# Exponent-bit terms of an attention kernel written by GpSimd in halves instead of by VectorE

## Chip, cores, metric

One core of one Trainium2 chip. The metric is device time of one execution, in microseconds, as a median over runs; shorter is better. A profile is one execution whose span is about 1.7 us shorter than the timed figure. All runs were in the fast state except the second of e4 (963.3 us, slow); the two single probe runs, e1 and e8, have no known state.

Terms: TensorE does the matmuls, ScalarE (ACT in the profiles) the exponentials and tanh, VectorE (DVE) and GpSimd (POOL) elementwise work. PSUM is the memory in which TensorE leaves its results, SBUF the working memory; to evict is to copy from PSUM to SBUF. The granted clock is the share of TensorE's full clock that the throttle let it have.

## The reference

A layer norm feeds two branches, and their sum is added to the input: attention with 16 heads of 28 columns over 2048 tokens, and a gated MLP (448 to 1792 to 448).

```python
def reference(A_x, A_wqkv, A_wo, B_x, B_w_gate, B_w_up, B_w_down):
    # _A_ref: q, k, v from xn @ wqkv; p = softmax(q k^T * Dh**-0.5); (p v) @ wo
    # _B_ref: (gelu(xn @ w_gate) * (xn @ w_up)) @ w_down
    x = A_x
    xn = _layernorm(x, axis=-1)
    return x + _A_ref(xn, A_wqkv, A_wo) + _B_ref(xn, B_w_gate, B_w_up, B_w_down)
```

## The kernel before

The scores of attention are made in 512 slots (two heads, 128 keys, 512 queries each), and each needs an exponential. ScalarE does 464 of them. The other 48 slots, two to a group, are done by VectorE with a trick: write `w = 128 * scale * log2(e) * score` as float16, then add a constant and convert to uint16; the bits, read as bfloat16, are a rough power of two. Five such terms with five constants are summed by TensorE, which multiplies each by the values. A group so costs VectorE two conversions from PSUM (`w`) and five terms.

```python
SHIFTS = (-2.74189, -2.62767, -2.43854, -2.23824, -1.98187)
...
    # keys of the groups in a sweep (two groups each), and the block that takes their terms
    D_AT = (((0, 4, 4), (8, 12, 12)), ((0, 4, 4), (8, 12, 12)), ((0, 4, 0), (5, 9, 0)))
...
    def emit_w(k):
        ...
        nc.vector.tensor_scalar(out=w_tiles[g][1][:, 2 * i * QT : 2 * (i + 1) * QT],
            in0=s_tiles.pop(k)[:], scalar1=128.0 * SCALE * LOG2E, scalar2=None, op0=ALU.mult)
...
    def emit_term(g, j):
        n, w = w_tiles[g]
        c = 128.0 * (127.0 + SHIFTS[j])
        if j == len(SHIFTS) - 1:
            bits = w[:].bitcast(U16)              # the last term overwrites w
        else:
            n = l_free.pop(0)[1]
            bits = ltile(n, [P, 4 * QT], U16, "t")[:]
        nc.vector.tensor_scalar(out=bits, in0=w[:], scalar1=c, scalar2=None, op0=ALU.add)
        ...
```

The order of all instructions comes from a planner inside the kernel. When the kernel is built, it plays the engines forward with a clock for each and with fixed costs, and emits whatever could start first. On the chip only the order and the data waits remain. TensorE fills planned gaps with filler matmuls (`jp`). VectorE also evicts PSUM and runs five gelu steps for each of 28 pieces of the MLP. Those five, all from SBUF to SBUF:

```python
T_EXP = 903; T_SWITCH = 100; PE_TO = 416; S_TO = 432; ACT_TO = 162; DVE_TO = 136; C_TS = 345; C_TERM = 608  # ns
...
            nc.vector.tensor_mul(st["a"][:], g[:], g[:])                     # two SBUF inputs
            nc.vector.tensor_scalar(out=st["a"][:], in0=st["a"][:], ...)     # one
            nc.vector.tensor_mul(st["a"][:], st["a"][:], g[:])               # two
            # tanh on ScalarE
            nc.vector.tensor_scalar(out=st["a"][:], in0=st["a"][:], ...)     # one
            nc.vector.tensor_mul(ht[:], st["a"][:], gu[:])                   # two
```

The softmax here doesn't subtract the row's maximum and nothing guards it: scores larger than these inputs give would overflow.

## Time and profile before

| | before |
|---|---|
| median of the first three runs | 487.17 us (487.15 to 488.54) |
| profiled span, granted TensorE clock | 485.5 us, 0.993 |
| ScalarE: first, last start of 492 large instructions | 13.8, 473.1 us |
| ScalarE: median spacing of starts | 904 ns |
| ScalarE: sum of spacing above 905 ns | 15.2 us, of it 12.8 us after 140 us |

The last three rows are worked out from the start times in the trace. ScalarE is the pacemaker: at 904 ns from start to start, the 491 intervals alone take 444 us.

From the page of the kernel before: busy time by engine, then the span in 40 slices (the busy share of a slice in tenths), then the chain of waits by engine.

```profile
PE 462.5 (95%) x3530; PEld 160.6 (33%) x3530; DVE 407.4 (84%) x728; ACT 463.4 (95%) x505; POOL 19.5 (4%) x74
...
DVE  6788999787469999999778999999986999776574
ACT  4899999999999999999999999999999999999992
POOL 4602020000000000000000000000000000000000
PEclk9999999999999999999999999999999999999997
...
PE 56%; DVE 28%; ACT 9%; issue 4%; POOL 1%; DMA 1%; DVEq 0%; ACTq 0%; POOLq 0%
```

ScalarE (ACT) is full from the second slice to the last but one, GpSimd (POOL) is empty from the eighth, and VectorE (DVE) is nearly full in several stretches. The groups view of the kernel before has line, engine, operation, output<-input, shapes and count, then busy us and mean ns of one, then idle time before it and its releaser:

```profile
L584 ACT ACTIVATE e<-st 128x1024 bf16<-128x1024 f32 x464 | 433.2, 1066 | 5.9 <-PE st L572 4.8 <-ACT e L584 0.3
L615 DVE TENSOR_SCALAR t<-w 128x2048 uint16<-128x2048 f16 x96 | 63.6, 684 | 0.2
L373 DVE TENSOR_TENSOR gl<-gl,g 128x1024 bf16<-128x1024 bf16 x28 | 19.2, 684 | 0.3
L615 DVE TENSOR_SCALAR w<-w 128x2048 uint16<-128x2048 f16 x24 | 16.6, 690 | 0.6
L367 DVE TENSOR_SCALAR gl<-gl 128x1024 bf16<-128x1024 bf16 x28 | 11.7, 418 | 0.1
```

The second and fourth lines are the work to be moved: 80.2 us. ScalarE idles before an exponential for only 5.9 us in all; the rest of its 15.2 us must be short delays hidden in overlapping durations. The table of stretches of the kernel before, before and after the first VectorE score groups, gives start:end, length, then the busy time of each engine:

```profile
13.80:140.00 126.20, 123.68 (x892) 45.52 (x891) 99.47 (x210) 125.98 (x137) 12.38 (x48) 1.00 0.21 59
140.00:475.00 335.00, 322.58 (x2556) 108.22 (x2555) 296.17 (x476) 329.72 (x356) 0.00 (x0) 1.00 0.11 31
```

The columns are PE, PEld, DVE, ACT, POOL, then granted clock, DMA share and GB/s. VectorE is busy 296 of 335 us in the second stretch.

### The profile page before, as it was taken

How to read it: one execution, taken by the hardware profiler on the slowest of the kernel's cores; microseconds unless marked ns; L12 is line 12 of the kernel's file. 1: busy time of each engine (PE TensorE's matmuls, PEld its weight loads, DVE VectorE, ACT ScalarE, POOL GpSimd, SP SyncE). 2: the span in 40 equal slices, each digit the busy share in tenths (PEclk: the TensorE clock that was granted, in tenths of full speed). 3: DMA queues.
4: the chain of work that ended last, by engine and by line, in shares of the span. 5: the costliest groups of instructions: out<-in, count | busy, mean ns of one | idle time of the engine just before them, and what ended most of it. 6: DMA issues, size and time to landing. Idle time of an engine off the chain costs nothing.

```text
span 485.5 us, 9277 instructions
## 1 busy us (share of the span) xinstructions
PE 462.5 (95%) x3530; PEld 160.6 (33%) x3530; DVE 407.4 (84%) x728; ACT 463.4 (95%) x505; POOL 19.5 (4%) x74
## 2 busy tenths in 40 slices
PE   8999999999999999999999999999999999999994
PEld 3343333333333332333333233323333333233221
DVE  6788999787469999999778999999986999776574
ACT  4899999999999999999999999999999999999992
POOL 4602020000000000000000000000000000000000
PEclk9999999999999999999999999999999999999997
DMA  6910112120011220120002022111001030000001
GB/s 165 311 36 20 39 39 61 36 57 20 2 42 38 77 61 19 40 58 21 1 1 60 28 70 62 40 53 40 3 1 39 30 87 3 1 2 1 2 1 38
DMA packets 41052, 20.71 MB, mean 43 GB/s; under 512 B 8240, under 2 KB 41008, under 8 KB 41008
## 3 DMA queue, kind: packets, MB, share of 16 engines
q1 hardware_dynamic: 40112, 19.68, 15.0%
q8 instruction: 27, 0.44, 0.4%
q10 hardware_dynamic: 896, 0.44, 0.3%
q14 instruction: 17, 0.14, 0.1%
HBM read 18.09 MB, written 1.84 MB: 41 GB/s over the span
## 4 chain that ended last, share of the span: by engine, by line
PE 56%; DVE 28%; ACT 9%; issue 4%; POOL 1%; DMA 1%; DVEq 0%; ACTq 0%; POOLq 0%
PE st L572 13%; PE gups L407 12%; PE ot L622 11%; PE op L469 10%; ACT e L584 8%; DVE t L615 4%; PE pp L309 4%; DVE w L594 4%; DVE g L393 3%; PE jp L985 3%; DVE gu L398 2%; PE pv L320 1%; DVE otsb L644 1%; DVE gl L363 1%; DVE st L211 1%
## 5 line engine op out<-in xcount | busy, mean ns | idle before, releaser
L584 ACT ACTIVATE e<-st 128x1024 bf16<-128x1024 f32 x464 | 433.2, 1066 | 5.9 <-PE st L572 4.8
L572 PE MATMUL st<-qT,kT 28*128 28x512 bf16 x1024 | 123.6, 383 | 2.9 <-ACT e L584 2.5
L622 PE MATMUL ot<-e,va 128*32 128x512 bf16 x928 | 92.4, 384 | 2.0 <-DVE gu L398 0.6
L572 PEld LDWEIGHTS <-kT 28*128 28x128 bf16 x1024 | 34.8, 91 | 110.5 <-issue 107.7
L594 DVE TENSOR_SCALAR w<-st 128x1024 f16<-128x1024 f32 x48 | 58.4, 1219 | 6.8 <-PE st L572 6.4
L615 DVE TENSOR_SCALAR t<-w 128x2048 uint16<-128x2048 f16 x96 | 63.6, 684 | 0.2
L407 PE MATMUL gups<-xnT,wu 112*128 112x512 bf16 x224 | 60.5, 380 | 2.3 <-DVE otsb L644 0.9
L407 PE MATMUL gups<-xnT,wg 112*128 112x512 bf16 x224 | 60.2, 381 | 0.6 <-DVE otsb L640 0.3
L622 PEld LDWEIGHTS <-va 128*32 128x32 bf16 x1408 | 34.1, 94 | 66.9 <-issue 55.6
L469 PE MATMUL op<-wd_sb,ht 128*128 128x448 bf16 x224 | 49.6, 354 | 0.4 <-DVE pre L497 0.2
L393 DVE CAST g<-gups 128x512 bf16<-128x512 f32 x56 | 38.2, 685 | 6.0 <-PE gups L407 5.9
L398 DVE TENSOR_TENSOR gu<-gups,g 128x512 bf16<-128x512 f32 x56 | 38.2, 685 | 3.1 <-PE gups L407 2.9
L644 DVE TENSOR_TENSOR otsb<-ot,otsb 128x512 f32<-128x512 f32 x45 | 30.8, 685 | 11.3 <-PE ot L622 10.9
L622 PE MATMUL ot<-t,va 128*32 128x512 bf16 x384 | 38.8, 384 | 0.4 <-DVE t L615 0.4
L377 ACT ACTIVATE gl<-gl 128x1024 bf16<-128x1024 bf16 x28 | 30.3, 1089 | 0.0
L407 PEld LDWEIGHTS <-wu 112*128 112x128 bf16 x224 | 19.4, 97 | 29.8 <-issue 14.7
L407 PEld LDWEIGHTS <-wg 112*128 112x128 bf16 x224 | 18.9, 97 | 28.7 <-issue 14.1
L469 PEld LDWEIGHTS <-ht 128*128 128x128 bf16 x224 | 18.9, 98 | 23.7 <-issue 10.3
L497 DVE TENSOR_TENSOR pre<-op,x 128x448 f32<-128x448 f32 x16 | 9.9, 621 | 18.0 <-PE op L469 18.0
L373 DVE TENSOR_TENSOR gl<-gl,g 128x1024 bf16<-128x1024 bf16 x28 | 19.2, 684 | 0.3
L389 DVE TENSOR_TENSOR ht<-gl,gu 128x1024 bf16<-128x1024 bf16 x28 | 19.1, 684 | 0.3
L363 DVE TENSOR_TENSOR gl<-g 128x1024 bf16<-128x1024 bf16 x28 | 19.1, 683 | 0.1
(105 smaller groups left out, 327.8 us busy)
## 6 DMA issues: line engine op xcount, KB each, us to landing
wg<-in_B_w_gate_dram SPq DMA_DIRECT2D x28, 224.0 KB
wu<-in_B_w_up_dram SPq DMA_DIRECT2D x28, 224.0 KB
out_dram<-res SPq DMA_DIRECT2D x15, 112.0 KB
wd_sb<-in_B_w_down_dram SPq DMA_DIRECT2D x1, 1568.0 KB
x<-in_A_x_dram SPq DMA_DIRECT2D x3, 448.0 KB
den<-otsb SPq DMA_DIRECT2D x60, 2.0 KB
rr<-recb SPq DMA_DIRECT2D x60, 1.0 KB
wst<-in_A_wqkv_dram SPq DMA_DIRECT2D x2, 392.0 KB
```

The source lines that it names most:

```text
L363: nc.vector.tensor_mul(st["a"][:], g[:], g[:])
L377: nc.scalar.activation(st["a"][:], st["a"][:], AF.Tanh, scale=TANH_SCALE)
L393: nc.vector.tensor_copy(g[:, k, :], ps[:])
L398: nc.vector.tensor_mul(gu[:, k, :], ps[:], g[:, k, :])
L407: nc.tensor.matmul(ps[:], lhsT=w[:, c, k * P : (k + 1) * P], rhs=xnc(Q, c), start=(c == 0), stop=(c == NDC - 1),)
L469: nc.tensor.matmul(ps[:, 0:D], lhsT=l, rhs=r, start=(n == 0), stop=(n == len(seq) - 1))
L572: nc.tensor.matmul(st[:, j * QT : (j + 1) * QT], lhsT=kT[(hg, kc // 4)][32 * hh : 32 * hh + Dh, (kc % 4) * P : (kc % 4 + 1) * P], rhs=qT[( ...
L584: nc.scalar.activation(e[:], s_tiles.pop(k)[:], AF.Exp, scale=SCALE)
L594: nc.vector.tensor_scalar(out=w_tiles[g][1][:, 2 * i * QT : 2 * (i + 1) * QT], in0=s_tiles.pop(k)[:], scalar1=128.0 * SCALE * LOG2E, scala ...
L615: nc.vector.tensor_scalar(out=bits, in0=w[:], scalar1=c, scalar2=None, op0=ALU.add)
L622: nc.tensor.matmul(ot[32 * hh : 32 * hh + 32, :], lhsT=vaug[kc][:, h * 32 : (h + 1) * 32], rhs=rhs, start=(b, hh) not in started, stop=las ...
L644: nc.vector.tensor_add(otsb[:], ot[:], otsb[:])
```

## The change

The intent: VectorE looks loaded and GpSimd idle, so GpSimd writes the terms, in halves of 1024 columns so that VectorE's gelu steps get a turn in between. The groups move to other keys of each sweep, to leave GpSimd time. The planner gets a clock for GpSimd (1030 ns for a half), does not plan a half and a gelu step at once, and several of its constants are re-tuned. The core of the diff, cut:

```diff
-T_SWITCH = 100
-PE_TO = 416
-S_TO = 432
-ACT_TO = 162
-DVE_TO = 136
+T_SWITCH = 104
+PE_TO = 430
+S_TO = 445
+ACT_TO = 180
+DVE_TO = 150
+POOL_TO = 150
+RAW = 85
+P_TERM = 1030
 ...
-    D_AT = (((0, 4, 4), (8, 12, 12)), ((0, 4, 4), (8, 12, 12)), ((0, 4, 0), (5, 9, 0)))
+    D_AT = (((0, 2, 8), (5, 8, 12)), ((0, 2, 8), (5, 8, 12)), ((0, 2, 0), (4, 6, 0)))
 ...
-    def emit_term(g, j):
+    def emit_term(g, j, i):
 ...
-        nc.vector.tensor_scalar(out=bits, in0=w[:], scalar1=c, scalar2=None, op0=ALU.add)
+        n, bits = t_tiles[g, j]
+        sl = slice(2 * i * QT, 2 * (i + 1) * QT)
+        nc.gpsimd.tensor_scalar(out=bits[:, sl], in0=w[:, sl], scalar1=c, scalar2=None, op0=ALU.add)
 ...
+    def pool_choice():          # when GpSimd's next half may start; it yields to a gelu step
+        ...
+        s = max(t, it[0], dve_lock[0])
+        d = dve_choice()
+        if d is not None and d[2][0] == 4 and d[0] < s + HOLD:
+            return None
+        return s, lambda: do_pool(it)
```

Not shown are other cost constants, the times at which gelu steps count as ready, and a rule at the end of the last block.

More of the change, by code (lines that the diff above doesn't have):

```diff
@@ L24 @@
 T_MM = 216
-T_SWITCH = 100
-PE_TO = 416
-S_TO = 432
-ACT_TO = 162
-DVE_TO = 136
+T_SWITCH = 104
[4 more added lines that the diff above has]
+POOL_TO = 150
 C_EVAC = 608
 C_TT = 600
-C_TS = 345
+C_TS = 335
+RAW = 85
 C_TERM = 608
 C_W = 1142
+P_TERM = 1030
 DMA_HOP = 5200
@@ L268 @@
     avail = {}
-    clock = {"PE": 0.0, "ACT": 0.0, "DVE": 0.0}
+    clock = {"PE": 0.0, "ACT": 0.0, "DVE": 0.0, "POOL": 0.0}
     dve_items = []
+    pool_items = []
     seq_n = [0]
@@ L275, in dve, with pool @@
         dve_items.append((cls, seq_n[0], ready, cost, f, keys))
+    def pool(ready, g, j, i):
+        seq_n[0] += 1
+        pool_items.append((ready, seq_n[0], g, j, i))
     def aux_tile(shape, dt, name):
@@ L288, in g_transpose @@
             if j == 0:
-                yield ("mm", 260)
+                yield ("mm", 268)
         yield (
-            "ev", 260, 1110, lambda: nc.vector.tensor_copy(xnT[t0 // 4][:, :, (t0 % 4) * P : (t0 % 4 + 2) * P], tp[0:DCH, :, :]),
+            "ev", 268, 1000, lambda: nc.vector.tensor_copy(xnT[t0 // 4][:, :, (t0 % 4) * P : (t0 % 4 + 2) * P], tp[0:DCH, :, :]),
             [("x", t0 // 4, t0 % 4 // 2)],
@@ L363, in f_sq @@
             nc.vector.tensor_mul(st["a"][:], g[:], g[:])
-            dve(4, 0, C_TS, f_poly)
+            dve(4, clock["DVE"] + C_TT + RAW, C_TS, f_poly)
         def f_poly():
@@ L369, in f_poly @@
             )
-            dve(4, 0, C_TT, f_arg)
+            dve(4, clock["DVE"] + C_TS + RAW, C_TT, f_arg)
         def f_arg():
@@ L383, in f_half @@
             )
-            st["half"] = True
+            st["half"] = clock["DVE"] + C_TS + RAW
             if st["gu"] == 2:
-                dve(4, 0, C_TT, f_h, [("ht", Q, pr)])
+                dve(4, st["half"], C_TT, f_h, [("ht", Q, pr)])
         def f_h():
@@ L394, in f_g @@
             if k == 1:
-                dve(4, 0, C_TT, f_sq)
+                dve(4, clock["DVE"] + C_EVAC + RAW, C_TT, f_sq)
         def f_gu(k, ps):
@@ L400, in f_gu @@
             if st["gu"] == 2 and "half" in st:
-                dve(4, 0, C_TT, f_h, [("ht", Q, pr)])
+                dve(4, clock["DVE"] + C_EVAC + RAW, C_TT, f_h, [("ht", Q, pr)])
         for w, f in ((wg, f_g), (wu, f_gu)):
@@ L605, with emit_term_dve @@
     term_ready = {}
-    def emit_term(g, j):
+    t_tiles = {}
+    NDT = 0
+    def emit_term_dve(g, j):
+        w = w_tiles[g][1]
+        n = l_free.pop(0)[1]
+        bits = ltile(n, [P, 4 * QT], U16, "t")[:]
+        nc.vector.tensor_scalar(
+            out=bits, in0=w[:], scalar1=128.0 * (127.0 + SHIFTS[j]), scalar2=None, op0=ALU.add
+        )
+        term_ready.setdefault(groups[g][2], []).append((clock["DVE"] + C_TERM + DVE_TO, g, n, bits))
+    def emit_term(g, j, i):
         n, w = w_tiles[g]
         c = 128.0 * (127.0 + SHIFTS[j])
-        if j == len(SHIFTS) - 1:
-            bits = w[:].bitcast(U16)
-        else:
-            n = l_free.pop(0)[1]
-            bits = ltile(n, [P, 4 * QT], U16, "t")[:]
-        nc.vector.tensor_scalar(out=bits, in0=w[:], scalar1=c, scalar2=None, op0=ALU.add)
-        term_ready.setdefault(groups[g][2], []).append((clock["DVE"] + C_TERM + DVE_TO, g, n, bits))
+        if i == 0:
+            if j < len(SHIFTS) - 1:
+                n = l_free.pop(0)[1]
+                t_tiles[g, j] = n, ltile(n, [P, 4 * QT], U16, "t")[:]
+            else:
+                t_tiles[g, j] = n, w[:].bitcast(U16)
+        n, bits = t_tiles[g, j]
+        sl = slice(2 * i * QT, 2 * (i + 1) * QT)
+        nc.gpsimd.tensor_scalar(out=bits[:, sl], in0=w[:, sl], scalar1=c, scalar2=None, op0=ALU.add)
+        if i == 1:
+            term_ready.setdefault(groups[g][2], []).append((clock["POOL"] + P_TERM + POOL_TO, g, n, bits))
     started = set()
@@ L829 @@
         for k in range(4):
-            ln_at_time(p0 + k, 640, lambda t=4 * g + k: ln_stats(t))
-        ln_at_time(p0 + 4, 500, lambda g=g: (ln_round(g), ln_std_newton(g)))
-        ln_at_time(p0 + 8, 180, lambda g=g: ln_rstd(g))
+            ln_at_time(p0 + k, 750, lambda t=4 * g + k: ln_stats(t))
+        ln_at_time(p0 + 4, 885, lambda g=g: (ln_round(g), ln_std_newton(g)))
+        ln_at_time(p0 + 8, 90, lambda g=g: ln_rstd(g))
         for k in range(4):
@@ L884, in do_s @@
             next_s[0] += 1
-        run_pe(start, "S", 216)
+        run_pe(start, "S", 227 if n == 2 else 222)
     def pv_choice():
@@ L896, in pv_choice @@
             best = (tr[0][0], "t")
-        if tail and not final[0] and len(sg["left"]) == 1:
-            return None
-        if sg["left"] and (sg["terms"] == 0 or len(sg["left"]) > 1):
+        if sg["left"] and not (tail and not final[0] and len(sg["left"]) == 1) and (sg["terms"] == 0 or len(sg["left"]) > 1):
             n, kc = sg["left"][0]
@@ L930, in do_pv @@
             l_free.append((start + 216 + PE_TO, n))
-            run_pe(start, "V", 216)
+            run_pe(start, "V", 226)
             return
@@ L938, in do_pv @@
             e_free[k] = start + 216 + 250
-        run_pe(start, "V", 222)
+        run_pe(start, "V", 226)
         if last:
@@ L1062, in dve_ok @@
         if isinstance(f, tuple) and f[0] == "t":
-            return f[2] == len(SHIFTS) - 1 or bool(l_free)
+            return bool(l_free)
         return True
@@ L1070, in dve_choice @@
             return None
+        if pool_run[0] <= t < pool_run[1]:
+            its = [it[:2] + (max(it[2], pool_run[1]),) + it[3:6] + (it,) if it[0] == 4 else it for it in its]
         ready = [it for it in its if it[2] <= t]
@@ L1079, in dve_choice @@
             it = min(its, key=lambda i: (i[2], i[0]))
-        return max(t, it[2]), lambda: do_dve(it)
+        return max(t, it[2]), lambda: do_dve(it), it
     def do_dve(it):
-        _, _, r, cost, f, keys = it
-        dve_items.remove(it)
-        start = clock["DVE"] = max(clock["DVE"], r)
+        cls, _, r, cost, f, keys = it[:6]
+        dve_items.remove(it[6] if len(it) > 6 else it)
+        start = max(clock["DVE"], r)
+        if cls == 4:
+            if pool_run[0] <= start < pool_run[1]:
+                start = pool_run[1]
+            dve_lock[0] = start + cost
+        clock["DVE"] = start
         end = start + cost
@@ L1093, in do_dve @@
                 if i == 1:
-                    dve(3, end, C_TERM, ("t", g, 0))
+                    dve_terms[g] = NDT
+                    for j in range(NDT):
+                        dve(4, end + RAW, C_TERM, ("t", g, j))
+                    pool(end + DVE_TO, g, NDT, 0)
             elif f[0] == "t":
-                _, g, j = f
-                emit_term(g, j)
-                terms_done[0] += 1
-                if j + 1 < len(SHIFTS):
-                    dve(3, end, C_TERM, ("t", g, j + 1))
+                emit_term_dve(f[1], f[2])
+                dve_terms[f[1]] -= 1
             else:
@@ L1108, in do_dve, with do_pool @@
         clock["DVE"] = end
+    HOLD = 300
+    dve_terms = {}
+    pool_run = [0.0, 0.0]
+    dve_lock = [0.0]
+    def pool_choice():
+        t = clock["POOL"]
+        its = [
+            it for it in pool_items if it[4] == 1 or (dve_terms[it[2]] == 0 if it[3] == len(SHIFTS) - 1 else l_free)
+        ]
+        if not its:
+            return None
+        it = min(its)
+        s = max(t, it[0], dve_lock[0])
+        d = dve_choice()
+        if d is not None and d[2][0] == 4 and d[0] < s + HOLD:
+            return None
+        return s, lambda: do_pool(it)
+    def do_pool(it):
+        pool_items.remove(it)
+        r, _, g, j, i = it
+        start = clock["POOL"] = max(clock["POOL"], r, dve_lock[0])
+        emit_term(g, j, i)
+        end = clock["POOL"] = start + P_TERM
+        pool_run[:] = [start, end]
+        j, i = j + i, 1 - i
+        if j < len(SHIFTS):
+            pool(end, g, j, i)
     def step():
@@ L1113, in step @@
             l_free.extend((0.0, n) for n in range(NL))
-        opts = [c for c in (act_choice(), pe_choice(), dve_choice()) if c is not None and c[0] < INF]
+        opts = [c for c in (act_choice(), pe_choice(), dve_choice(), pool_choice()) if c is not None and c[0] < INF]
         if not opts:
@@ L1123 @@
         pass
-    assert next_a[0] == len(a_slots) and not (todo or urgent or lazy or mid[0] or dve_items or tanh_q)
+    assert next_a[0] == len(a_slots) and not (todo or urgent or lazy or mid[0] or dve_items or pool_items or tanh_q)
     final[0] = True
@@ L1139 @@
     preload(2)
+    assert segs[-1]["terms"] == 0
     while segs[-1]["left"]:
```

## The prediction

> **What bounds the kernel now.** ScalarE. The groups view gives 464 exponentials of 128x1024, and 28 tanh. They overlap: in the timeline, consecutive starts are 904 ns apart in the median. The first starts at 13.8 us and the last at 473.1 us, so 491 intervals take 459.3 us; at 0.904 us each they would take 443.9 us. ScalarE therefore loses about 15.2 us to late inputs, of which 12.8 us lie after 140 us (where VectorE score groups begin) and 2.4 us before. Outside the stream there are 13.8 us of head and about 12 us of tail. The page shows TensorE 95% busy (closely matched, with 41 filler matmuls), VectorE 84%, GpSimd 4%. In the windows view VectorE is 88% busy from 140 to 475 us and 97 to 99% busy in 40 us stretches there. The chain of waits puts 28% on VectorE: its late evictions make ScalarE's inputs late. At 188 to 192 us VectorE runs five terms in a row, TensorE nine filler matmuls, and ScalarE idles 0.7 us.
>
> **What changes.** The counts of exponentials, tanh and useful matmuls are the same in the built program; filler matmuls fall from 41 to 5. VectorE loses 120 terms of 128x2048: 96 x 684 ns + 24 x 690 ns = 80 us. Its load after 140 us falls from 296 us to about 216 us of 335 (65%). GpSimd gains 240 halves of 128x1024. From this trace's GpSimd copies (one element 0.18 us, 448 columns 0.56 us) I estimate 1.0 to 1.1 us each, so about 250 us, some 20.6 us for each of the twelve sweeps of about 28 us: GpSimd becomes 70 to 80% busy there, tight but not the limit.
>
> The Trainium skill ("SBUF — State Buffer", Who interferes with whom) says that a VectorE instruction in a two-port mode, or with two SBUF inputs against a GpSimd instruction that reads SBUF, excludes GpSimd for the whole instruction. No run here shows it yet. The gelu steps on VectorE (28 x (3 x 0.684 + 2 x 0.418) us = 81 us, about 60 us of it after 140 us) are of that kind. 250 + 60 = 310 of 335 us fits barely. The schedule plans around it, but no semaphore enforces the plan, so I expect gelu steps and halves to delay each other, 20 to 40 us over all on VectorE, mostly absorbed.
>
> **How much counts.** Not 80 us: VectorE is not the bound. Only the ScalarE gaps after 140 us can go, 12.8 us at most. From 100 to 140 us, where VectorE is 61% busy, the gaps still cost about 0.5 us per 20 us (TensorE granularity, tanh spacing). At that rate the rest would lose 8 us, so about 4.6 us are gained; re-tuned planning constants may add one. The head and tail stay.
>
> **Predicted time: 481.5 us, range 475 to 488.** Faster by over 2%: 0.20; within 2%: 0.72; slower by over 2%: 0.08.
>
> **What would show it right or wrong.** VectorE busy about 330 to 370 us instead of 407 (more than 327 means stretched gelu steps: look at the mean of gelu multiplies, now 684 ns). GpSimd about 250 to 300 us; a half of 1.0 to 1.2 us. ScalarE start spacing still 904 ns in the median, with the excess falling from 15 to about 9 us.
>
> **What would make it wrong.** If halves take over 1.3 us, because of exclusion or conversion, GpSimd needs over 310 us and terms arrive late: accumulation blocks stay open, exponential buffers fill, and ScalarE stalls every sweep (490 us and more). If gelu steps queue behind several halves, evictions behind them hold up TensorE. If instead nearly all gaps vanish, the floor is about 474 us.

## The result, and the profile after

| | before | after |
|---|---|---|
| median | 487.16 us (4 runs) | 821.65 us (821.29 to 821.77, 4 runs) |
| ratio | | 1.685 (1.682 to 1.688) |
| span, granted clock | 485.5 us, 0.993 | 819.5 us, 0.765 |
| ScalarE: spacing above 905 ns, after 140 us | 12.8 us | 339.4 us |

A ratio is the mean time of one kernel's fast runs over that of the other's fast runs in the same rounds, so it is not quite the ratio of the medians. Results are correct in both.

The same lines of the page, of the changed kernel:

```profile
PE 575.6 (70%) x3494; PEld 167.6 (20%) x3494; DVE 371.7 (45%) x608; ACT 472.4 (58%) x505; POOL 681.2 (83%) x314
...
DVE  6889786632647323318342484313244721402132
ACT  6999999833657437327454384454364743823531
POOL 5101001999999999999999999999999999998993
PEclk9999999965877678658767776876587756875765
...
POOL 72%; PE 15%; issue 9%; DVE 2%; DMA 1%; ACT 0%; POOLq 0%; DVEq 0%; ACTq 0%
```

GpSimd is now full from the first score group to the end, and is 72% of the chain that ended last. ScalarE falls to about half. The groups view of the changed kernel:

```profile
L638 POOL TENSOR_SCALAR t<-w 128x1024 uint16<-128x1024 f16 x192 | 530.6, 2789 | 76.3 <-DVE w L602 76.3
L592 ACT ACTIVATE e<-st 128x1024 bf16<-128x1024 f32 x464 | 442.6, 1078 | 323.6 <-PE st L580 322.7
L638 POOL TENSOR_SCALAR w<-w 128x1024 uint16<-128x1024 f16 x48 | 132.5, 2775 | 0.0
L646 PE MATMUL ot<-t,va 128*32 128x512 bf16 x384 | 69.8, 457 | 156.2 <-POOL t L638 154.5 <-DVE gu L406 0.5 <-DVE g L401 0.5
L646 PE MATMUL ot<-w,va 128*32 128x512 bf16 x96 | 27.6, 576 | 66.4 <-POOL w L638 66.4
L381 DVE TENSOR_TENSOR gl<-gl,g 128x1024 bf16<-128x1024 bf16 x28 | 26.0, 930 | 0.5
L375 DVE TENSOR_SCALAR gl<-gl 128x1024 bf16<-128x1024 bf16 x28 | 18.0, 642 | 0.2
```

A half takes 2.79 us in the mean, not 1.0 to 1.1. TensorE waits 221 us (154.5 + 66.4) for terms, and ScalarE waits 323 us for scores that TensorE cannot make meanwhile. The gelu steps are longer too (930 for 684 ns, 642 for 418 ns). The spread of the halves, from the view of line 638 of the changed kernel (minimum/median/maximum ns):

```profile
L638 POOL TENSOR_SCALAR t<-w x192: 2760/2763/3102, 141.4 to 798.9; 128x1024 uint16<-128x1024 f16 x192
```

Minimum and median are 3 ns apart. A duration made by collisions with VectorE would scatter; this one looks like the instruction's own. The stretches of the changed kernel, in the columns shown before:

```profile
13.80:140.00 126.20, 124.14 (x875) 45.57 (x877) 102.76 (x214) 125.44 (x137) 12.66 (x49) 1.00 0.22 60
140.00:805.00 665.00, 433.30 (x2535) 114.68 (x2529) 258.00 (x353) 339.09 (x356) 659.57 (x240) 0.72 0.06 15
```

Little changes before 140 us. After it GpSimd is busy 660 of 665 us: 240 halves x 2.763 us are 663 us. TensorE's granted clock is 0.72 in this stretch, in which it often idles.

### The profile page after: what moved, and what is told of

It reads as the page before. It is cut to its first block, busy times and chain, and to the rows that moved or that the text cites. A ratio compares the mean times of both kernels' runs of the same rounds, so it can differ in the third digit from the quotient of the medians.

```text
span 819.5 us, 9379 instructions
## 1 busy us (share of the span) xinstructions
PE 575.6 (70%) x3494; PEld 167.6 (20%) x3494; DVE 371.7 (45%) x608; ACT 472.4 (58%) x505; POOL 681.2 (83%) x314
## 4 chain that ended last, share of the span: by engine, by line
POOL 72%; PE 15%; issue 9%; DVE 2%; DMA 1%; ACT 0%; POOLq 0%; DVEq 0%; ACTq 0%
POOL t L638 61%; POOL w L638 10%; PE gups L415 4%; PE st L580 3%; PE ot L646 2%; PE pp L317 2%; PE pv L328 1%; PE op L477 1%; POOLq L1271 0%; DVE g L401 0%; DMA x<-in_A_x_dram 0%; PE tp L293 0%; DVE st L214 0%; PE jt L674 0%; POOL na L249 0%
## 5 line engine op out<-in xcount | busy, mean ns | idle before, releaser
L592 ACT ACTIVATE e<-st 128x1024 bf16<-128x1024 f32 x464 | 442.6, 1078 | 323.6 <-PE st L580 322.7
L638 POOL TENSOR_SCALAR t<-w 128x1024 uint16<-128x1024 f16 x192 | 530.6, 2789 | 76.3 <-DVE w L602 76.3
L646 PE MATMUL ot<-t,va 128*32 128x512 bf16 x384 | 69.8, 457 | 156.2 <-POOL t L638 154.5
L580 PE MATMUL st<-qT,kT 28*128 28x512 bf16 x1024 | 138.7, 445 | 5.8 <-DVE w L602 4.7
L638 POOL TENSOR_SCALAR w<-w 128x1024 uint16<-128x1024 f16 x48 | 132.5, 2775 | 0.0
L646 PE MATMUL ot<-e,va 128*32 128x512 bf16 x928 | 118.2, 470 | 1.1 <-DVE pre L505 0.5
L646 PE MATMUL ot<-w,va 128*32 128x512 bf16 x96 | 27.6, 576 | 66.4 <-POOL w L638 66.4
L415 PE MATMUL gups<-xnT,wg 112*128 112x512 bf16 x224 | 69.9, 430 | 2.7 <-DVE gu L406 0.7
L415 PE MATMUL gups<-xnT,wu 112*128 112x512 bf16 x224 | 71.0, 433 | 0.9 <-DVE gu L406 0.2
L477 PE MATMUL op<-wd_sb,ht 128*128 128x448 bf16 x224 | 59.5, 399 | 0.7 <-DVE otsb L668 0.6
```

Source lines behind the costliest of these rows:

```text
L415: nc.tensor.matmul(ps[:], lhsT=w[:, c, k * P : (k + 1) * P], rhs=xnc(Q, c), start=(c == 0), stop=(c == NDC - 1),)
L477: nc.tensor.matmul(ps[:, 0:D], lhsT=l, rhs=r, start=(n == 0), stop=(n == len(seq) - 1))
L580: nc.tensor.matmul(st[:, j * QT : (j + 1) * QT], lhsT=kT[(hg, kc // 4)][32 * hh : 32 * hh + Dh, (kc % 4) * P : (kc % 4 + 1) * P], rhs=qT[( ...
L592: nc.scalar.activation(e[:], s_tiles.pop(k)[:], AF.Exp, scale=SCALE)
L638: nc.gpsimd.tensor_scalar(out=bits[:, sl], in0=w[:, sl], scalar1=c, scalar2=None, op0=ALU.add)
L646: nc.tensor.matmul(ot[32 * hh : 32 * hh + 32, :], lhsT=vaug[kc][:, h * 32 : (h + 1) * 32], rhs=rhs, start=(b, hh) not in started, stop=las ...
```

## The experiments

Theory A: the add alone, as GpSimd executes it, takes 2.76 us for 1024 columns, and that rate is the whole slowdown. Rivals: (B) VectorE and GpSimd hold each other up at SBUF; (C) the moved groups, the constants or an order planned for a wrong rate. "Before" was run beside every call, with medians of 486.9 to 487.1 us.

| run | median us | ratio to before (95%) |
|---|---|---|
| e2, halves on VectorE | 499.2 | 1.025 (1.022 to 1.028) |
| e3, engine only | 1001.5 | 2.055 (2.050 to 2.060) |
| e4, planned with 2400 ns | 945.8 (and 963.3, slow) | no ratio |
| e5, two operations | 519.6 | 1.065 (1.063 to 1.067) |
| e6, two operations, 1110 ns | 522.6 | 1.073 (1.071 to 1.074) |
| e7, engine only, two operations | 577.2 | 1.186 (1.182 to 1.189) |
| e9, write only (wrong results) | 492.9 | 1.013 (1.009 to 1.017) |
| e10, positions only | 490.6 | 1.007 (1.004 to 1.009) |
| e11, all but the engine | 495.6 | 1.016 (1.014 to 1.019) |
| e12, constants only | 495.9 | 1.020 (1.016 to 1.024) |
| e13, free terms (wrong results) | 489.5 | 1.007 (1.003 to 1.010) |
| e14, last term only | 511.1 | 1.048 (1.045 to 1.051) |

The two probe runs, e1 and e8, have no time that is of interest.

### e1: the disputed instruction by itself

Appended to the kernel before, after its last store, four times each (cut):

```diff
+    ge.tensor_scalar(out=pu16[:, h], in0=pf16[:, h], scalar1=16000.0, scalar2=None, op0=A)
+    ge.tensor_scalar(out=qf32[:], in0=pf32[:], scalar1=16000.0, scalar2=None, op0=A)
+    ge.tensor_scalar(out=pbf[:, h2], in0=pbf[:, h], scalar1=16000.0, scalar2=None, op0=A)
+    ge.tensor_scalar(out=pu16[:, h], in0=pf16[:, h], scalar1=2.0, scalar2=16000.0, op0=ALU.mult, op1=A)
+    ge.tensor_copy(pu16[:, h], pf16[:, h])
+    ...    # other widths and types; then ten halves beside VectorE multiplies and tensor-scalars
```

> The kernel before, with GpSimd instructions appended after its last store, four of each form, VectorE idle; then ten halves while VectorE runs gelu-like steps. Theory 1 (number conversion: the float16-to-uint16 form itself is slow on GpSimd): float16 to uint16 over 1024 columns takes 2.76 us alone too, while float32 to float32 and bfloat16 to bfloat16 take about 1.0 to 1.1 us. Theory 2 (the tensor-scalar operation is slow in any number type): every tensor-scalar form over 1024 columns takes about 2.7 us, only copies take about 1.0. Theory 3 (exclusion by VectorE at the shared memory port): the half takes 1.0 to 1.1 us alone, and 2.7 us only beside VectorE.

From the groups view of this run (line 1224 is the form with two operations; all the other tensor-scalar lines add alone):

```profile
L1204 POOL TENSOR_SCALAR pu<-pf 128x1024 uint16<-128x1024 f16 x4 | 11.1, 2772 | 422.3 <-issue 422.1
L1212 POOL TENSOR_SCALAR qf<-pf 128x1024 f32<-128x1024 f32 x4 | 11.1, 2767 | 0.2
L1216 POOL TENSOR_SCALAR pbf<-pbf 128x1024 bf16<-128x1024 bf16 x4 | 11.1, 2767 | 0.2
L1224 POOL TENSOR_SCALAR pu<-pf 128x1024 uint16<-128x1024 f16 x4 | 4.2, 1047 | 0.2
L1230 POOL CAST pu<-pf 128x1024 uint16<-128x1024 f16 x4 | 4.2, 1038 | 0.3
```

With VectorE idle, the add alone takes the same 2.77 us. B is out as the cause of the 2.76 us. Number types do not matter either: eight combinations gave 2.767 to 2.772 us, so number conversion, the first of the three theories stated, falls. "Tensor-scalar is slow in any type" fits these lines but not the last form: multiply and add together take 1.05 us, like a copy. None of the stated theories had foreseen that **one** operation costs 2.6 times **two**. The copies on which my prediction's estimate rested do take 1.04 us at 1024 columns; they were the wrong stand-in.

### e2: the same order, halves on VectorE

```diff
-        nc.gpsimd.tensor_scalar(out=bits[:, sl], in0=w[:, sl], scalar1=c, scalar2=None, op0=ALU.add)
+        nc.vector.tensor_scalar(out=bits[:, sl], in0=w[:, sl], scalar1=c, scalar2=None, op0=ALU.add)
```

> The changed kernel, its plan, positions and constants untouched, with only the 240 halves issued by VectorE in the place of GpSimd. If GpSimd's rate alone makes the slowdown: a half takes about 0.42 us on VectorE, 101 us in all, VectorE carries about 317 of 335 us after 140 us, and the time returns to 485 to 505 us. If the moved score groups or the re-tuned planning constants make it: it stays above 700 us.

Measured: 499.2 us, a half 0.417 us in the median. One word takes back 322 of 334 us, so neither positions nor constants nor order can make the slowdown. The granted clock returns to 0.982: the low clock came with the slow halves. It isn't the cause either, since e4 below is slower still at 0.905.

### e3 and e4: engine alone, and a plan with another rate

e3 is the kernel before with `nc.gpsimd` for `nc.vector` in `emit_term`; e4 is the changed kernel with

```diff
-P_TERM = 1030
+P_TERM = 2400
```

> The kernel before, its plan and score positions untouched, with only the 120 whole terms (2048 columns) issued by GpSimd. If GpSimd's rate alone makes the slowdown: a term takes about 5.4 us (twice 2.76 less one fixed part), 650 us in all, and the time is 800 to 840 us, as in the changed kernel. If the positions or the plan make it: below 600 us.

> The changed kernel, planned with 2400 ns for a half instead of 1030 ns (the planner finds no complete order at the measured 2763 ns). If throughput of GpSimd is the limit, no order helps: 240 x 2.763 = 663 us from about 140 us on, so 800 to 830 us again. If the order, made for a wrong rate, costs the time: below 700 us.

Both missed upwards, at 1001 and 946 us. e3 shows that the engine alone is enough for the slowdown, and that the new positions, plan and halves, taken together, help: in e3 GpSimd idles 264 us before terms, 255 us of it waiting for VectorE's `w`, where the changed kernel has 76 us of such idle time, nearly all of it before the first half. In e4, GpSimd idles 199 us before terms, 98 us of it waiting for TensorE, and the planner puts in 750 filler matmuls (306 us busy) where the changed kernel has 5. Knowing more of the rate made the plan worse, not better. At this rate no order can go below 663 us of halves, but an order can waste more.

### e5 and e6: the same term in the fast form

```diff
-        nc.gpsimd.tensor_scalar(out=bits[:, sl], in0=w[:, sl], scalar1=c, scalar2=None, op0=ALU.add)
+        nc.gpsimd.tensor_scalar(out=bits[:, sl], in0=w[:, sl], scalar1=1.0, scalar2=c, op0=ALU.mult, op1=ALU.add)
```

e6 is e5 with `P_TERM = 1110`.

> The changed kernel with each half written as multiply by 1.0, then add the constant, in the place of the add alone; plan and positions untouched, results the same. If the one-operation form is what is slow: a half falls from 2.76 us to about 1.1 us (1.11 us in the probe of the two-operation form), GpSimd carries 240 x 1.11 = 266 us, and the time falls to that which the prediction gave for such a half, 475 to 488 us. If GpSimd beside the gelu steps of VectorE, or the order of issue, is a limit of its own: still above 500 us.

> The same as the two-operation run, but planned with 1110 ns for a half, the rate of the probe, in the place of 1030 ns. If the plan must know the rate: 2 to 5 us faster than the two-operation run planned with 1030 ns. If the time follows the gaps that are there whatever the plan: within 2 us of it, either way.

e5: 519.6 us, correct. The median half falls from 2763 to 1045 ns and 302 us are gone. This shows theory A for 302 of the 334 us, by a change that touches nothing but the form. It is not the whole slowdown: the time is not the 475 to 488 us that I expected of such a half; 32.6 us remain. e6, at 522.6 us, is 3 us slower, outside both of its cases, so telling the planner 1110 ns does not help. (The 1.11 us of these two expectations is a quarter of the 4.44 us from the first start to the last end of the four probes in e1, gaps included; one of them takes 1.05 us.)

The timeline of e5 between 285 and 294 us (start, duration, instruction, idle time before it) shows a piece of the rest:

```profile
285.71 8.79 POOL L638 TENSOR_SCALAR t<-w 128x1024 uint16<-128x1024 f16 x7 [8.60 <-PE ot L646]
285.79 1.50 DVE L397 TENSOR_TENSOR ht<-gl,gu 128x1024 bf16<-128x1024 bf16 x1
287.21 1.52 DVE L371 TENSOR_TENSOR gl<-g 128x1024 bf16<-128x1024 bf16 x1
288.76 1.15 DVE L375 TENSOR_SCALAR gl<-gl 128x1024 bf16<-128x1024 bf16 x1
289.95 1.40 DVE L381 TENSOR_TENSOR gl<-gl,g 128x1024 bf16<-128x1024 bf16 x1
291.27 0.68 DVE L668 TENSOR_TENSOR otsb<-ot,otsb 128x512 f32<-128x512 f32 x1
...
292.00 0.43 PE L415 MATMUL gups<-xnT,wu 112*128 112x512 bf16 x1 [2.83 <-DVE otsb L668]
...
293.07 1.02 ACT L592 ACTIVATE e<-st 128x1024 bf16<-128x1024 f32 x1 [3.06 <-PE st L580]
```

GpSimd runs seven halves without a pause, at 1.26 us each instead of 1.05, and each of four gelu steps takes 0.7 us or more longer than its 0.68 or 0.42 us. The eviction `otsb` stands behind them in VectorE's queue, TensorE waits 2.83 us for that PSUM bank, and ScalarE idles 3.06 us. The planner had meant these halves and steps to take turns, but nothing in the program enforces it: GpSimd starts a half as soon as its data are there.

### e7: engine alone, in the fast form

This is e3 with the two-operation form, whole terms of 2048 columns.

> The kernel before, plan and positions untouched, with only the 120 whole terms on GpSimd in the two-operation form; by the probe about 2.0 to 2.1 us each, 250 us in all. If GpSimd's rate was all that was wrong with the engine move: below 520 us. If the plan, made for terms of 0.6 us on VectorE, has to be made anew for the slower engine: 540 us or more, since each group's five terms take 10 us in a row in the place of 3.4 us and hold up the accumulation.

Measured: 577.2 us, the second case; a term takes 1.90 us in the median. Against e5's 519.6 us, the positions, the plan and the halves of the change, taken together, are worth 58 us once GpSimd writes all terms.

### e8: which forms are fast, and both engines at once

The same probes with other forms, and sixteen fast halves beside VectorE.

> The kernel before with GpSimd forms appended, alone, then sixteen two-operation halves beside gelu-like steps on VectorE. If it is the number of operations: add alone, multiply alone and maximum alone take about 2.8 us, and every pair about 1.1 us. If it is the multiply-then-add pair alone that has a fast way: add then multiply and add then add take 2.8 us or more. Beside VectorE: if the two engines exclude each other for whole instructions, a VectorE multiply of 0.68 us takes up to 1.1 us more; if the port is held for part of a half only, about 0.3 us more, as with the slow halves.

From its groups view, in this order: add; multiply, add; add, multiply; add, add; multiply; maximum. The last two lines are VectorE's multiplies and tensor-scalars, run beside fast halves.

```profile
L1204 POOL TENSOR_SCALAR pu<-pf 128x1024 uint16<-128x1024 f16 x4 | 11.1, 2772 | 423.8 <-issue 423.5
L1206 POOL TENSOR_SCALAR pu<-pf 128x1024 uint16<-128x1024 f16 x4 | 4.2, 1050 | 0.3
L1208 POOL TENSOR_SCALAR pu<-pf 128x1024 uint16<-128x1024 f16 x4 | 4.2, 1047 | 0.3
L1210 POOL TENSOR_SCALAR pu<-pf 128x1024 uint16<-128x1024 f16 x4 | 14.5, 3632 | 0.3
L1212 POOL TENSOR_SCALAR pu<-pf 128x1024 uint16<-128x1024 f16 x4 | 11.1, 2773 | 0.3
L1214 POOL TENSOR_SCALAR pu<-pf 128x1024 uint16<-128x1024 f16 x4 | 11.1, 2766 | 0.3
...
L1233 DVE TENSOR_TENSOR pa<-pb,pc 128x1024 bf16<-128x1024 bf16 x8 | 11.4, 1426 | 0.2
L1235 DVE TENSOR_SCALAR pa<-pb 128x1024 bf16<-128x1024 bf16 x8 | 9.2, 1144 | 0.3
```

Both theories on forms are half right: the three single operations tried are slow, and of the three pairs tried one multiply with one add is fast, in either order, while add with add is the slowest of all. Beside VectorE, a multiply takes 1.43 us for 0.68, and a tensor-scalar 1.14 us for 0.42. That is 0.7 us more each, inside the "up to 1.1 us" of whole-instruction exclusion and well above the 0.3 us of partial holding.

### e9: GpSimd writes, but does not read (wrong results on purpose)

The control for B: same plan, about the same time on GpSimd, but the halves no longer read.

```diff
-        nc.gpsimd.tensor_scalar(out=bits[:, sl], in0=w[:, sl], scalar1=c, scalar2=None, op0=ALU.add)
+        lo = 2 * i * QT
+        nc.gpsimd.tensor_copy(bits[:, lo : lo + 1], w[:, lo : lo + 1])
+        nc.gpsimd.memset(bits[:, sl], 16256)
```

> Wrong results on purpose. The changed kernel, where each half is a one-column copy from w (it keeps the waits) and then a memset of the 1024 columns: GpSimd writes as much, but reads almost nothing. About 1.1 us a half, as in the two-operation run (519.6 us). If the 32 us that are left there come from gelu steps of VectorE and reading halves holding each other up: gelu steps fall from 116 us in all towards 81 us, and the time falls to 485 to 500 us. If they come from the latency of terms on GpSimd or from the order of the plan: within 5 us of 519.6 us.

Measured: 492.9 us, 26.7 us less than e5, with GpSimd busy 290.7 us against e5's 289.7 us. From its groups view:

```profile
L381 DVE TENSOR_TENSOR gl<-gl,g 128x1024 bf16<-128x1024 bf16 x28 | 19.2, 686 | 0.5
L375 DVE TENSOR_SCALAR gl<-gl 128x1024 bf16<-128x1024 bf16 x28 | 15.5, 552 | 0.2
```

In e5 these two means are 978 and 765 ns. Summed over their five lines, the gelu steps are busy 80.7 us before, 116.3 us in e5 and 88.7 us in e9. The multiplies are back at their own time and the tensor-scalars not quite (552 for 418 ns; no run shows which mode they are in). That fits the Trainium skill, "SBUF — State Buffer", Who interferes with whom: GpSimd work that only writes does not hold up a VectorE instruction with two SBUF inputs, but does hold up one in a two-port mode. So about 27 of e5's 32.6 us go away with GpSimd's reads, and the gelu steps lose 27.6 us of stretch with them. One rival is not excluded: e9 also gives TensorE constants in the place of terms, and its granted clock is 0.977 to 0.995 where e5 has 0.956 to 0.972. But e2, with the same plan and right results, reaches 0.976 to 0.986 as well, so the clock doesn't need the constants. That leaves 6 us.

### e10, e11, e12: the parts of the change that are not the engine

e10 is the kernel before with the new `D_AT` alone. e11 is the changed kernel with whole terms planned and issued on VectorE as before (positions, constants and gelu readiness stay). e12 is e11 with the old `D_AT`.

> The kernel before with only the positions of the score groups moved to those of the change, terms on VectorE. If positions matter little, as the prediction assumed: 485 to 490 us. If groups that stand closer together overload VectorE: 492 us or more.

> Everything of the change (positions, re-tuned constants, readiness of the gelu steps) but the engine: whole terms on VectorE, and planned there. With the plan for VectorE made anew, 485 to 492 us if the plan is no worse than before; near the 499 us of the halves on VectorE if positions and constants, not the extra work of halves, cost those 12 us.

> The re-tuned constants and gelu readiness alone: positions as before, whole terms on VectorE. If the constants describe the chip better: 482 to 487 us. If they don't: 487 to 492 us.

They measured 490.6, 495.6 and 495.9 us; e10 and e11 fell between their two cases, and e12 missed both of its ranges by 4 us. The last start of a large ScalarE instruction is at 473.4, 473.2 and 474.2 us in their profiles, and before at 473.1 us. So the stream of exponentials ends within 1.1 us of before's; the tail is longer: from that start to the end of the span before takes 12.4 us, e10 14.0, e11 20.9 and e12 19.2 us. In the timeline of e11, TensorE still has MLP output work when the exponentials end:

```profile
472.32 4.20 PE L477 MATMUL op<-wd_sb,ht 128*128 128x448 bf16 x14
...
478.68 2.81 PE L477 MATMUL op<-wd_sb,ht 128*128 128x448 bf16 x14 [0.71 <-DVE pre L530]
```

In e11's order that low-priority work did not fit in front of the end. In e9 the tail is 14.6 us and the last start is at 475.4 us, which is 2.2 and 2.3 us worse than before: in its profile that is the 6 us, less the spread of the runs. What makes it is not shown: besides positions, constants and order, the gelu steps of e9 are still stretched by 8 us.

### e13: terms that cost nothing (wrong results on purpose)

Does relief of VectorE gain anything at all? The kernel before, planned anew with no terms issued; TensorE multiplies a fixed tile as often.

```diff
-        nc.vector.tensor_scalar(out=bits, in0=w[:], scalar1=c, scalar2=None, op0=ALU.add)
+        bits = kT[(0, 0)][:]                     # some constant tile
 ...
-                    dve(3, end, C_TERM, ("t", g, 0))
+                    dve(3, end, 0, ("t", g, 0))     # and so for the terms after it
```

> Wrong results on purpose. The kernel before with its own positions and constants, planned anew with terms that cost nothing and are not issued at all: TensorE multiplies the same number of times, by a fixed tile. This is the most that taking the terms off VectorE could ever give, with no other engine burdened. If VectorE's load makes the gaps of ScalarE after 140 us, as the prediction said: its excess there falls from 12.8 us to about 8 us or less, and the time to 482 us or less. If the gaps come from elsewhere (TensorE's own sequence): 485 to 489 us, excess as before.

Measured: 489.5 us (488.3 to 495.3). The stretch after 140 us, in the columns shown before:

```profile
140.00:475.00 335.00, 322.91 (x2539) 108.22 (x2540) 224.54 (x350) 325.88 (x352) 0.00 (x0) 0.97 0.11 31
```

VectorE is at 224.5 of 335 us (296.2 before), and nothing is gained. ScalarE's 445th large instruction starts at 426.7 us, against 428.6 us before, so by then 1.9 us had been gained: the spacing above 905 ns between 140 us and that start sums to 8.9 us, against 10.8 us before. Most of the gaps stay when the terms are gone. From 430 to 460 us TensorE's granted clock was 0.72, and the gain was lost there; over the whole run the excess after 140 us is 18.0 us, so both cases of the expectation missed it. Why the clock fell there, the runs do not tell. It was 0.970 to 0.989 in all six runs, against 0.992 to 0.999 in the kernel before beside them, and what that alone cost is not known. In this plan the relief is worth some 2 us up to there, and nothing in the end.

### e14: one term of five on GpSimd

The kernel before; the last term of each group in the fast form on GpSimd, whole, planned as 2100 ns that cost VectorE nothing.

> The kernel before with only the last of each group's five terms on GpSimd, whole, in the two-operation form (24 x about 2.0 us), planned so; VectorE loses 16 us. If a small share avoids most of the mutual holding and VectorE's load matters: 484 to 486.5 us, faster than both kernels. If relief of VectorE buys nothing: 487 to 490 us.

Measured: 511.1 us, 24 us slower with only 24 instructions moved. It missed both expectations. The planner of before knows no exclusion, and the timeline of the first such term shows it in a pure form:

```profile
155.33 1.91 POOL L617 TENSOR_SCALAR w<-w 128x2048 uint16<-128x2048 f16 x1 [86.05 <-DVE t L620]
155.51 2.26 DVE L390 TENSOR_TENSOR ht<-gl,gu 128x1024 bf16<-128x1024 bf16 x1
...
157.70 0.68 DVE L394 CAST g<-gups 128x512 bf16<-128x512 f32 x1
...
158.43 0.58 PE L439 MATMUL bt<-rr,sel 128*128 128x512 bf16 x1 [1.60 <-DVE g L394]
...
161.17 1.02 ACT L585 ACTIVATE e<-st 128x1024 bf16<-128x1024 f32 x1 [2.03 <-PE st L573]
```

The gelu multiply starts 0.18 us after GpSimd's term and ends 0.53 us after the term's end: all but 0.15 us of its own 0.68 us lies behind GpSimd's term. The eviction behind it is late, TensorE waits 1.6 us, and ScalarE 2.0 us. No version tried here beats the kernel before.

## Why the prediction was wrong

- **The failing step** is "From this trace's GpSimd copies (one element 0.18 us, 448 columns 0.56 us) I estimate 1.0 to 1.1 us each, so about 250 us", and after it "tight but not the limit". A half took 2.76 us, and GpSimd 663 us. e1 shows that this is the form's own cost, with VectorE idle and in every type tried; e8 finds it for multiply and maximum too; e5 shows that the form alone carries 302 us of the 334. The estimate was right for a copy, and for multiply with add (1.05 us); I took one operation's rate for another's without a record of it. The kernel before had no wide tensor-scalar on GpSimd, so its trace could not give the number, and the range should have said so.
- **"If halves take over 1.3 us, ... (490 us and more)"** named the right mechanism: terms late, blocks open, ScalarE stalled. It named neither the size nor a fair chance of it.
- **"20 to 40 us over all on VectorE, mostly absorbed"**: with halves at the predicted rate (e5) the stretch was 116.3 - 80.7 = 35.6 us, as predicted. It was not absorbed: e9 against e5 puts its cost at about 27 us. A gelu step that is held holds the PSUM evictions behind it, and TensorE and ScalarE follow.
- **"About 4.6 us are gained"** from a lighter VectorE: no run shows it. With the terms gone altogether (e13) the stream was 1.9 us ahead at 427 us, 8.9 of the 10.8 us of gaps up to there were still there, and the time was no better. VectorE's 28% in the chain of waits did not mean that less VectorE work ends sooner. That TensorE's own sequence makes the remaining gaps is likely (in e13 ScalarE waits 9.9 of its 10.6 us before exponentials for TensorE's scores), but not shown.
- **"Not 80 us"**, "the head stays" and "TensorE closely matched" held. "Re-tuned planning constants may add one" had the wrong sign with the terms on VectorE: e12 is 1.6 to 2.4% slower, nearly all of it in the tail, so "the tail stays" failed there as well.

The sum, in the order in which the runs take it apart: 487 before; + 6 for positions, constants, order and what GpSimd's writes still hold up, not told apart (e9); + 27 for GpSimd's reads, by the gelu steps that they hold (e5 - e9); + 302 for the one-operation form (after - e5); = 822 us. What is left open: why a single operation or add with add is slow on GpSimd (no run looks inside it), and whether some other order could turn e13's head start into time.

## What to carry to other kernels

Before moving work to another engine, time that very instruction form there, alone; a neighbouring form's rate can be off by 2.6 times. Where two engines can hold each other, look at what queues behind the held instruction (in both timelines above an eviction, then TensorE, then ScalarE), and test with a control that keeps the time and takes away the collision. And before relieving an engine, run the version in which its work is free: if that gains nothing, as here, expect little from any placement under the same plan.

## What the Trainium skill lacked or had wrong

- "GPSIMD Engine Reference", 4.1 Engine selection, has one-input elementwise work on GpSimd at roughly line rate. The runs agree for copies (1.04 us for 1024 columns) and for a tensor-scalar of one multiply and one add (1.05 us), but a single add, multiply or maximum takes 2.77 us and add with add 3.63 us. No page that I found says that the rate hangs on the pair of operations.
- "SBUF — State Buffer", Who interferes with whom, says that a VectorE instruction with two SBUF inputs, or in a two-port mode, is shut out for a reading GpSimd instruction's whole length when that one came first. The fast form agrees: 2.26 us for a 0.68 us multiply beside a 1.91 us term (e14). For multiplies the slow form does not: beside halves of 2.76 us the longest took 1.61 us, 0.93 us more than its own time. In e3, beside whole slow terms of 5.36 us, all 19 multiplies that were held for over 0.2 us ended 1.19 us before a term did (the longest took 4.15 us), so they ran during its last part; the 18 tensor-scalars so held all ended 0.28 us after a term (the longest took 5.57 us for its 0.42 us). The probes agree: multiplies take 0.98 us in the mean beside slow halves (e1), 1.43 us beside fast ones (e8).
